# Attention weights of the last twelve units brought to keys by tokens through DRAM instead of TensorE transposes

## The chip, the cores and the metric

The kernel runs on one core of a Trainium2 chip. The metric is the device time of one execution in microseconds (us). Three runs of the kernel before gave a median of 1243.5 us (1242.62 to 1245.04).

## The reference

Three layers follow each other, all in float32. An attention over eight batches and eight heads pools its keys and values by 8 first, so that 576 queries meet 72 keys. Its output, 4608 tokens by 512 features, goes through a feed-forward layer with an ELU (512 to 2048 to 512), and that one's through a second with a softmax-weighted activation and a layer norm (512 to 1024 to 512).

```python
k_p = k.reshape(B, H, Sp, 8, D).mean(axis=3); v_p = v.reshape(B, H, Sp, 8, D).mean(axis=3)
scores = scale * q @ k_p.T
attn = exp(scores - max(scores)); attn = attn / (sum(attn) + 1e-9)
x = (attn @ v_p) as [4608, 512]
h = x @ w_in;  x = elu(h) @ w_out
h = x @ w_in2; solu = h * softmax(h); ln = (solu - mean) / sqrt(var + 1e-6) * g_ln
out = ln @ w_out2
```

## The kernel before

**Units.** The attention is done in 32 units, a unit being one batch and two heads (128 features). Four units make the 576 tokens of a batch. Unit i has the tiles q and k (128 features by 576 tokens) and v (72 keys by 128 features by 8). `att_setup` reduces k and v over the pool of 8 on VectorE (`att_kr`, line 477, and `att_vr`, line 496) and scales k on ScalarE into two diagonal blocks (`att_kc`, lines 487 and 488). `att_scores` (line 514) multiplies five blocks of 128 tokens with them; the fifth block is the last 128 of the 576 tokens and overlaps the fourth by 64. The result is ten groups of 72 scores for each of 128 tokens (two heads, five blocks; tile "es"). VectorE takes maximum and difference (lines 533, 535), ScalarE the exponential (542), VectorE the sum and its reciprocal (558 to 561), GpSimd multiplies (563).

**Keys by tokens.** The product with v needs the weights with keys on the partitions. `att_T(i, 0)` transposes the first head's four groups on TensorE into PSUM (line 573), and ScalarE copies them to the tile "a" (574). `att_T(i, 1)` does the second head's four and then the fifth block of both heads (lines 573, 574, 578, 580). `att_V` multiplies "a" with the pooled v, 64 features of one head at a time, in pieces that end at a block of 512 tokens (line 599). `att_x` brings the result to DRAM (tensor x0d) by a ScalarE copy and a DMA (613, 614), for tokens from 1536 on.

**Where the units run.** Tokens go in nine blocks of 512. The first feed-forward layer does the first three blocks as plain products (`m_h1`, `m_o1`: lines 975 and 1030), and the other six in three pairs by a form of Strassen's product with seven products in place of eight (`h_step`, line 1170, and `o_step`, line 1260). Each product there is six matmuls of 512 columns. A pair has 56 products in `h_step` and 28 steps of two in `o_step`. Every product takes one weight tile of 256 KB from a ring of 14 (`w_ring`, tile "wr", line 1162). The third pair has no attention beside it; the second layer (`z_mul`, `z_out`, lines 1367 and 1505) follows.

Attention steps are spread over the products: `att_half(n)` is called with a growing n, four steps a unit. With i = n // 4, step 0 does scores, maximum and exponential of unit i; step 1 the sums of unit i and `att_T(i - 1, 1)`; step 2 `att_V(i - 1)`, `att_x(i - 1)` and `att_setup(i + 1)`; step 3 `att_T(i, 0)`. The counter `credit` grows with each product so that the steps up to `upto(...)` are done when the outputs of `o_step` 4 are. Units 20 to 27 fall into the first pair, 28 to 31 into the second. While the last steps of a pair's `o_step` run, `sx_next` loads the next pair's blocks from x0d (line 1116, tiles sA, su, sP) and builds their sums, differences and splits into two parts (lines 1079, 1080).

**The order.** Everything up to the second layer is put in order by the planner `settle` before the program is built. It gives each instruction a cost, follows the five queues in time, and writes each engine's order down; the chip then works in that order. TensorE's products keep the order of the program, but one that is not ready may be passed by up to ten later ones (`WINDOW`). VectorE and ScalarE take what is due first. All DMAs are issued from SyncE's one queue, in the planned order; a DMA that waits there holds those behind it. Tiles have a fixed number of buffers ("es" 3, "a" 2, "cv" 2, PSUM tag "C" 2).

The second layer has a round trip through DRAM of the kind that the change uses: VectorE transposes blocks of 32 by 32 (`t_dve`, line 1454), a DMA writes them to the tensor zd (`t_store`, 1459), four DMAs bring them back with features on the partitions (`t_load`, 1466), and ScalarE and VectorE read the loaded tile in runs of 32 elements (1474, 1478).

Of the kernel before, what the change touches and what calls it, by code (L numbers as in the profile page):

```python
# [8 lines left out]
F32 = mybir.dt.float32  # L9
# [329 lines left out]
def kernel(  # L339
# [15 lines left out]
    nc = tc.nc  # L355
    P = 128
    NB, NP, _, S = qT.shape
    SK = v.shape[2]
# [12 lines left out]
    sb = ctx.enter_context(tc.tile_pool(name="sb", bufs=2))  # L371
    ps = ctx.enter_context(tc.tile_pool(name="ps", bufs=2, space=bass.MemoryType.PSUM))
    dr = ctx.enter_context(tc.tile_pool(name="dr", bufs=1, space=bass.MemoryType.DRAM))
    att = ExitStack()
    pa = att.enter_context(tc.tile_pool(name="pa", bufs=2, side="right"))
    first = ExitStack()
    p1 = first.enter_context(tc.tile_pool(name="p1", bufs=2))

    x0d = dr.tile([P, KDM, NT], F32, name="x0d")
    x1d = dr.tile([P, KDM, NT], F32, name="x1d")  # L380
    w1d = dr.tile([P, NF // 2, 7, 2, 256], F32, name="w1d")
    w3d = dr.tile([P, 7, NF // 2, 2, 256], F32, name="w3d")
    w2d = dr.tile([P, 7, 4, 512], F32, name="w2d")
    o2d = dr.tile([P, 2, 2, 4, 512], F32, name="o2d")
    zd = [dr.tile([4, P, 256], F32, name=f"zd{i}") for i in range(4)]
    ident = cst.tile([P, P], F32, name="ident")
    make_identity(nc, ident)
# [13 lines left out]
    starts = [512 * j for j in range(NBLK)]  # L401
    units = [(b, p) for b in range(NB) for p in range(NP)]
    NU = len(units)
    QT = (0, P, 2 * P, 3 * P, S - P)
    NG = 2 * len(QT)

    GROUPED = (1,2)
    NTREE = 3
    KPOOL = ()
    NPOOL = ()  # L410

    xh, xl = {}, {}
    gate = {}

    def xblk(j):
        if j not in xh:
            xh[j] = xtile(f"xh{j}")
            xl[j] = xtile(f"xl{j}")
        return xh[j], xl[j]
# [3 lines left out]
    st = {}  # L423
# [26 lines left out]
    def pool_tree(dst, src):  # L450
        n = POOL // 2
        while n > 1:
            nc.gpsimd.tensor_tensor(src[:, :, 0:n], src[:, :, 0:n], src[:, :, n:2 * n], op=ALU.add)
            n //= 2
        nc.gpsimd.tensor_tensor(dst, src[:, :, 0], src[:, :, 1], op=ALU.add)
# [25 lines left out]
    def att_kc(i):  # L481
        kp, kr = att_kv(i)[0], st.pop(("kr", i))
        if i in KPOOL:
            nc.gpsimd.tensor_scalar(kp[0:64, 0:SK], kr[0:64, :], 1.0 / (8 * POOL), None, op0=ALU.mult)
# [5 lines left out]
    def att_vr(i):  # L490
        v_t = st["kq", units[i][1]][2] if i < NP else st["ld", i][1]
        vr = att_kv(i)[1]
        if i < NTREE:
            pool_tree(vr, v_t)
# [3 lines left out]
    def att_setup(i):  # L498
        for part in (att_kr, att_kc, att_vr):
            part(i)  # L500

    def bc(x, m):
        return x.rearrange("p (a o) -> p a o", o=1).to_broadcast([P, m, SK])

    def att_scores(i, banks):

        kp, vt = st["kp", units[i][0], units[i][1]]
        q_t = st.pop(("q", i))
        st["sv", i] = []
        for t0, t1 in ((0, 2), (2, 4)) if i < NP else ((0, 3), (3, 5)):  # L510
            s = next(banks)
            ts = QT[t0:t1]
            for t, o in enumerate(ts):
                nc.tensor.matmul(  # L514
                    s[:, t * 2 * SK:(t + 1) * 2 * SK], q_t[:, o:o + P], kp, start=True, stop=True
                )
            m = 2 * len(ts)
            st["sv", i].append((2 * t0, m, s[:, 0:m * SK].rearrange("p (a k) -> p a k", k=SK)))
            yield
        st["a", i] = (pa.tile([P, NG, SK], F32, name=f"es{i}", tag="es", bufs=3), vt)  # L520

    def grouped(i):
        return i in GROUPED
# [1 line left out]
    def small(name):  # L525
        return pa.tile([P, NG], F32, name=name, tag="mx", bufs=4)

# [23 lines left out]
    def att_soft(i):  # L551
        es, vt = st["a", i]
        n = 2 * NP if i < NP else NG
        es = es[:, 0:n]
# [10 lines left out]
    def att_T(i, h):  # L565

        es, vt = st["a", i]
        if h == 0:
            st["aT", i] = pa.tile([SK, 2, S], F32, name=f"a{i}", tag="a")
        a = st["aT", i]  # L570
        pt = ps.tile([P, 512], F32, name=f"pt{i}_{h}", tag="C")
        for t in range(4):
            nc.tensor.transpose(pt[0:SK, t * P:(t + 1) * P], es[:, 2 * t + h, :], ident)  # L573
        nc.scalar.copy(a[:, h, 0:4 * P], pt[0:SK, :])
        if h == 1 and i >= NP:
            pr = ps.tile([P, 512], F32, name=f"pr{i}", tag="C")
            for g in range(2):
                nc.tensor.transpose(pr[0:SK, g * P:(g + 1) * P], es[:, 8 + g, :], ident)  # L578
            lo = 5 * P - S
            nc.scalar.copy(  # L580
                a[:, :, 4 * P:S], pr[0:SK, 0:2 * P].rearrange("s (g t) -> s g t", g=2)[:, :, lo:P]
            )

    def att_V(i, banks):

# [48 lines left out]
    def rest(part):  # L634

        kz = st["kz"]
        if part == 0:
            s = ps.tile([P, 512], F32, name="rs", tag="C")
            for p in range(NP):
                nc.tensor.matmul(  # L640
                    s[RW * (p % 2):RW * (p % 2) + RW, (p // 2) * 2 * SK:(p // 2 + 1) * 2 * SK],
                    kz[:, p, qr], kz[:, p, 0:2 * SK], start=True, stop=True,
                )
            es = st["rest"] = pa.tile([P, NG, SK], F32, name="esr", tag="es", bufs=3)[:, 0:NP]
            mx = small("mxr")[:, 0:NP]
            sv = s[:, 0:NP * SK].rearrange("p (a k) -> p a k", k=SK)
            nc.vector.tensor_reduce(mx, sv, axis=AX, op=ALU.max)
            nc.vector.tensor_tensor(es, sv, bc(mx, NP), op=ALU.subtract)
            nc.scalar.activation(es, es, AF.Exp)
        elif part == 1:  # L650
            es = st["rest"]
            sm = small("smr")[:, 0:NP]
            nc.vector.tensor_reduce(sm, es, axis=AX, op=ALU.add)
            nc.vector.tensor_scalar(sm, sm, 1e-9, float(POOL), op0=ALU.add, op1=ALU.mult)
            nc.vector.reciprocal(sm, sm)
            nc.gpsimd.tensor_tensor(es, es, bc(sm, NP), op=ALU.mult)
        elif part == 2:
            es = st.pop("rest")
            pt = ps.tile([P, 512], F32, name="ptr", tag="C")
            for g in range(NP):  # L660
                nc.tensor.transpose(pt[0:SK, g * P:(g + 1) * P], es[:, g, :], ident)
            st["rest"] = kz[0:SK, :, qr.stop:qr.stop + P]
            nc.scalar.copy(st["rest"], pt[0:SK, :].rearrange("s (g t) -> s g t", t=P))
        else:
            a = st.pop("rest")
            pv = ps.tile([P, 512], F32, name="pvr", tag="C")
            for p in range(NP):
                for h in range(2):
                    d = slice(64 * h, 64 * h + 64)
                    o = RW * (p % 2)  # L670
                    nc.tensor.matmul(
                        pv[d, p * RW:(p + 1) * RW], kz[0:SK, p, 2 * SK + 64 * h:2 * SK + 64 * h + 64],
                        a[:, 2 * (p // 2) + h, o:o + RW], start=True, stop=True,
                    )
            th, tl = (x[:, :, 0:RW] for x in xblk(1))
            src = pv[:, 0:NP * RW].rearrange("p (a t) -> p a t", t=RW)
            nc.scalar.copy(th, src)
            nc.vector.tensor_tensor(tl, src, th.bitcast(F32), op=ALU.subtract)

    def single():  # L680
        while True:
            yield ps.tile([P, 512], F32, name="at", tag="C")
# [2 lines left out]
        for _ in range(2):  # L685
            yield ps.tile([P, 512], F32, name="at2", tag=tag, bufs=4 if tag == "A" else 2)

    NSTEP = 4 * NU + 3
    nload = [0]

    def att_half(n):

        while nload[0] < min(NU, n // 4 + 3):
            att_load(nload[0])
            nload[0] += 1
        i, r = divmod(n, 4)
        before = NP <= i - 1
        if r == 0:
            if i < NU:
                for _ in att_scores(i, single()):  # L700
                    pass
                att_max(i)
                att_exp(i)
        elif r == 1:
            if i < NU:
                att_soft(i)
            if before:
                att_T(i - 1, 1)
        elif r == 2:
            if before:  # L710
                att_V(i - 1, single())
                att_x(i - 1)
            if i + 1 < NU:
                att_setup(i + 1)
        elif r == 3:
            if i < NU:
                att_T(i, 0)


# [828 lines left out]
    def startup():  # L1548
# [28 lines left out]
        def T(i):  # L1577
            att_T(i, 0)
            att_T(i, 1)
# [133 lines left out]
    def upto(j):  # L1713

        i = ((512 * (j + 1) - 1) // S) * NP + NP - 1
        return min(NSTEP, 4 * i + 7)

    goal = [upto(1), (upto(1) + upto(4)) // 2 // 4 * 4 + 3, upto(4)]
    def combo_all():
# [78 lines left out]
    pu = third.enter_context(tc.tile_pool(name="pu", bufs=1, reuse_waits="tile"))  # L1798
    prs = [4, 5, 6, 7]

    for pr in range(NTP):
        c = NPL + 2 * pr
# [216 lines left out]
    before = None  # L2019
    for key, n in seq:  # L2020
        k = (key, n)
# [18 lines left out]
        before = k  # L2040
    for n, (a, b) in enumerate(map(tiles_of, range(NPAIR))):
        if n > 1:
            c = n // 2
# [3 lines left out]
            x = [("xl", c) if c > 1 else "x1", ("S4", n - 2)]  # L2047
# [80 lines left out]
```

## Time and profile before

| | |
|---|---|
| Median of the runs | 1243.5 us |
| Profiled execution, its own time | 1244.2 us |
| Span, first to last instruction | 1242.4 us |
| TensorE busy | 1231.6 us (99%) |
| VectorE busy | 980.7 us (79%) |
| ScalarE busy | 823.1 us (66%) |
| GpSimd busy | 173.9 us (14%) |
| DMA moved | 263.31 MB, 212 GB/s |

PE is TensorE's matmul, PEld its weight load, DVE VectorE, ACT ScalarE, POOL GpSimd, SPq SyncE's queue. TensorE's matmuls overlap in the records: the duration of one is longer than the distance from its start to the next one's, so a price is read from starts. A "x" with a number is the count of instructions in a row. The clock is a share of full speed.

### The profile page before, as it was taken

To read this page: it belongs to the slowest core of one execution; us is meant where nothing else is said; L and a number is where in the kernel's file an instruction comes from. 1 tells how busy PE (TensorE), PEld (TensorE's weight loads), DVE (VectorE), ACT (ScalarE), POOL (GpSimd) and SP (SyncE) were. 2 spreads that over 40 slices of the span, in tenths; PEclk is the share of its full clock that TensorE was granted. 3 is DMA by queue.
4 is the path that set the end of the run, shared out by engine and by line. 5 is a ranking of instruction groups with operands and counts; after the bars stand their busy time and mean duration, and the time that the engine had idled before them with its cause. 6 is when DMAs were issued, how large, how long until landed. Compare 5 with 4: busy or idle time off the path is not lost.

```text
span 1242.4 us, 17361 instructions
## 1 busy us (share of the span) xinstructions
PE 1231.6 (99%) x5824; PEld 996.5 (80%) x5824; DVE 980.7 (79%) x1487; ACT 823.1 (66%) x1378; POOL 173.9 (14%) x148
## 2 busy tenths in 40 slices
PE   8999999999999999999999999999999999999998
PEld 6777787777787878788888788888888888888887
DVE  7898888888777789866788587996788787878763
ACT  7978666566667775557774477753676776767664
POOL 3554323332210010000000000000000000000000
PEclk9999999999999999999999999999999999999999
DMA  8877666676657878697766888788545444554341
GB/s 287 258 222 256 196 199 217 220 267 222 220 182 225 251 219 250 210 303 215 206 204 217 283 277 270 251 273 320 202 153 170 161 132 157 168 155 144 110 151 53
DMA packets 172841, 263.31 MB, mean 212 GB/s; under 512 B 16336, under 2 KB 88528, under 8 KB 171728
## 3 DMA queue, kind: packets, MB, share of 16 engines
q1 hardware_dynamic: 172752, 262.21, 66.2%
q8 instruction: 46, 0.75, 0.2%
q14 instruction: 43, 0.35, 0.1%
HBM read 182.46 MB, written 79.69 MB: 211 GB/s over the span
## 4 chain that ended last, share of the span: by engine, by line
PE 97%; ACT 1%; DVE 1%; POOL 0%; DMA 0%; issue 0%; ACTq 0%
PE po L1505 16%; PE hA L1170 16%; PE oA L1260 12%; PE h L975 10%; PE o L1030 10%; PE zX L1367 8%; PE zZ L1367 4%; PE oC L1260 4%; PE at L514 3%; PE at L599 3%; PE hB L1170 3%; PE oB L1260 3%; PE pt L573 2%; PE zY L1367 2%; PE pr L578 0%; PE busy L1575 0%
## 5 line engine op out<-in xcount | busy, mean ns | idle before, releaser
L1505 PE MATMUL po<-w,dhl 128*128 128x512 f32 x864 | 203.7, 392 | 0.0
L1505 PEld LDWEIGHTS po<-w,dhl 128*128 128x128 f32 x864 | 162.2, 188 | 35.1
L1260 PE MATMUL oA<-op,wr 128*128 128x512 f32 x672 | 158.2, 392 | 0.0
L1260 PEld LDWEIGHTS oA<-op,wr 128*128 128x128 f32 x672 | 125.1, 188 | 30.1 <-issue 2.9
L1250 ACT CAST op<-g 128x1024 fp32r<-128x1024 f32 x84 | 87.9, 1052 | 63.4 <-PE oA L1260 29.3
L1251 DVE TENSOR_TENSOR op<-g,op 128x1024 fp32r<-128x1024 f32 x84 | 102.6, 1227 | 24.8 <-ACT op L1250 24.3
L1170 PE MATMUL hA<-sS,wr 128*128 128x512 f32 x414 | 103.7, 392 | 0.0
L1367 PE MATMUL zX<-w,xh 128*128 128x512 f32 x288 | 100.8, 392 | 0.0
L1445 POOL TENSOR_TENSOR sc<-sc,mhalf 128x1 f32<-128x1 f32 x36 | 20.9, 586 | 558.3 <-DVE sc L1444 295.3
L896 POOL TENSOR_TENSOR wol<-wo,woh 128x512 fp32r<-128x512 f32 x48 | 75.6, 1578 | 135.7 <-ACT woh L895 122.9
L563 POOL TENSOR_TENSOR es<-es,sm 128x720 f32<-128x720 f32 x28 | 45.4, 1621 | 329.0 <-DVE sm L561 237.6
L1170 PEld LDWEIGHTS hA<-sS,wr 128*128 128x128 f32 x414 | 77.0, 188 | 17.8 <-issue 1.4
L975 PE MATMUL h<-xh,wh 128*128 128x512 f32 x192 | 78.6, 409 | 0.1
L1030 PE MATMUL o<-gh,woh 128*128 128x512 f32 x192 | 78.7, 410 | 0.0
L975 PE MATMUL h<-xh,wl 128*128 128x512 f32 x192 | 75.4, 393 | 0.7 <-POOL wl L792 0.7
L975 PE MATMUL h<-xl,wh 128*128 128x512 f32 x192 | 75.3, 392 | 0.0
L1030 PE MATMUL o<-gh,wol 128*128 128x512 f32 x192 | 75.1, 391 | 0.0
L1182 ACT COPY sp<-hA 128x512 f32<-128x512 f32 x72 | 42.2, 586 | 38.5 <-PE hA L1170 38.2
L1190 DVE SCALAR_TENSOR_TENSOR g<-ep,g 128x512 f32<-128x512 f32 x72 | 51.3, 717 | 17.7 <-ACT ep L1189 17.3
L1367 PEld LDWEIGHTS zX<-w,xh 128*128 128x128 f32 x288 | 54.1, 188 | 12.3
L1377 ACT COPY sn<-zX 128x512 f32<-128x512 f32 x54 | 31.7, 587 | 48.1 <-PE zX L1367 47.8
L1189 ACT ACTIVATE ep<-ep 128x512 f32<-128x512 f32 x96 | 59.1, 630 | 1.8
(374 smaller groups left out, 2817.3 us busy)
## 6 DMA issues: line engine op xcount, KB each, us to landing
wr<-w3d SPq DMA_DIRECT2D x168, 256.0 KB
wr<-w1d SPq DMA_DIRECT2D x161, 256.0 KB
raw<-in_w SPq DMA_DIRECT2D x32, 512.0 KB
dT<-zd SPq DMA_DIRECT2D x128, 128.0 KB
v<-in_v SPq DMA_DIRECT2D x32, 288.0 KB
x1r<-x1d SPq DMA_DIRECT2D x9, 1024.0 KB
out<-ot SPq DMA_DIRECT2D x36, 256.0 KB
raw<-in_w SPq DMA_DIRECT2D x8, 1024.0 KB
```

The source lines that it names most:

```text
L563: eng.tensor_tensor(es, es, bc(sm, n), op=ALU.mult)
L896: nc.gpsimd.tensor_tensor(ol, t[:, f % 4, :], oh.bitcast(F32), op=ALU.subtract)
L975: nc.tensor.matmul(h[:, 0:n], a[g][:, kk, fo:fo + P], x[j][:, kk, 0:n], start=(kk == 0 and m == 0), stop=(kk == KDM - 1 and m == 2), skip_ ...
L1030: nc.tensor.matmul(acc, a[:, dm * P:(dm + 1) * P], x[:, 0:n], start=(f == 0 and m == 0), stop=(f == NF - 1 and m == 2))
L1170: nc.tensor.matmul(bank, w[:, a, kk], x[:, b, kk], start=(start and m == 0), stop=(stop and m == 5), skip_group_check=True,)
L1189: gate["act"] = nc.scalar.activation(e, e, AF.Exp, scale=-1.0).ins
L1190: gate["dve"] = nc.vector.scalar_tensor_tensor(d, e, 1.0, h, op0=ALU.subtract, op1=ALU.max).ins
L1250: gate["act"] = nc.scalar.copy(o[:, 0], src).ins
L1251: gate["dve"] = nc.vector.tensor_tensor(o[:, 1], src, o[:, 0].bitcast(F32), op=ALU.subtract).ins
L1260: nc.tensor.matmul(banks[d], ws[i][:, a, d * P:(d + 1) * P], o[:, b, i], start=(start and t == 0 and i == 0 and m == 0), stop=(stop and t ...
L1367: nc.tensor.matmul(bank, x[:, o:o + P], w[:, y + k, :], start=(start and m == 0), stop=(stop and m == 5), skip_group_check=True,)
L1505: nc.tensor.matmul(po, a[:, c], b[c // 4][:, c % 4, :], start=(m == 0), stop=(m == 3 * NC2 - 1))
```

## The change

For units 20 to 31 `att_T` and `att_V` are replaced by two functions. `att_D(i)` takes its place at step 3 of unit i. It has VectorE transpose three blocks of 32 keys (0 to 31, 32 to 63, 64 to 95, of which the last has 8 keys) for all ten groups; each is written to DRAM and read back into "a", with keys on the partitions and tokens in an order of 32-token parts. `att_VB(i - 1)` comes at step 3 of unit i, one step later than `att_V` did, ahead of `att_D(i)`. It multiplies in that order, and three ScalarE copies put the tokens back; the first 512 and the last 64 tokens go to x0d in two DMAs. `att_setup(i + 1)` moves from step 2 to step 3 where unit i - 1 is one of these. The number of steps grows by one. The tile "es" gets 24 columns more, which GpSimd clears for these units, and "a" has room for 640 tokens.

```diff
+    ed = [dr.tile([3, P, NG * 32], F32, name=f"ed{i}") for i in range(3)]
+    BLOCKT = range(20, 32)
...
-        st["a", i] = (pa.tile([P, NG, SK], F32, name=f"es{i}", tag="es", bufs=3), vt)
+        e = pa.tile([P, NG * SK + 24], F32, name=f"es{i}", tag="es", bufs=3)
+        if i in BLOCKT:
+            nc.gpsimd.memset(e[:, NG * SK:], 0.0)
+        st["a", i] = (e[:, 0:NG * SK].rearrange("p (g k) -> p g k", k=SK), vt)
...
-            st["aT", i] = pa.tile([SK, 2, S], F32, name=f"a{i}", tag="a")
+            st["aT", i] = pa.tile([SK, 2, 5 * P], F32, name=f"a{i}", tag="a")
...
+    def att_D(i):
+        es, vt = st["a", i]
+        part, g, k = (list(x) for x in es.ap)
+        a = st["aT", i] = pa.tile([SK, 2, 5 * P], F32, name=f"a{i}", tag="a")
+        av = a.rearrange("k h t -> k (h t)").rearrange("k (r x) -> k r x", r=4)
+        for b in range(3):
+            n = min(32, SK - 32 * b)
+            et = pu.tile([P, NG, 32], F32, name=f"et{i}", tag="et", bufs=2)
+            nc.vector.transpose(et, bass.AP(es.tensor, es.offset + 32 * b * k[0], [part, g, [k[0], 32]]))
+            nc.sync.dma_start(out=ed[i % 3][b], in_=et.rearrange("p g c -> p (g c)"))
+            nc.sync.dma_start(
+                out=av[32 * b:32 * b + n], in_=ed[i % 3][b].rearrange("(r f) x -> f r x", r=4)[0:n]
+            )
+
+    def att_VB(i, banks):
+        es, vt = st.pop(("a", i))
+        a = st.pop(("aT", i)).rearrange("k h t -> k (h t)").rearrange("k (r t h c) -> k h r t c", r=4, h=2, c=32)
+        b, p = units[i]
+        x = sb.tile([P, 512], F32, name="xr", tag="cv", bufs=2)
+        y = sb.tile([P, 512], F32, name="xr", tag="cv", bufs=2)[:, 0:S - 512]
+        xv = x.rearrange("p (t r c) -> p t r c", r=4, c=32)
+        for r, n in ((0, 4), (2, 5)):
+            pv = next(banks)
+            for h in range(2):
+                d = slice(64 * h, 64 * h + 64)
+                nc.tensor.matmul(pv[d, 0:64 * n], vt[:, d], a[:, h, r:r + 2, 0:n], start=True, stop=True)
+            o = pv[:, 0:64 * n].rearrange("p (r t c) -> p t r c", r=2, c=32)
+            st["pv", i, r] = o
+        for r, n in ((0, 4), (2, 5)):
+            o = st.pop(("pv", i, r))
+            nc.scalar.copy(xv[:, :, r:r + 2], o[:, 0:4])
+            if n > 4:
+                nc.scalar.copy(y.rearrange("p (r c) -> p r c", c=32), o[:, 4])
+        for t, lo, hi in ((x, 0, 512), (y, 512, S)):
+            gate["x0"] = nc.sync.dma_start(out=x0d[:, p, b * S + lo:b * S + hi], in_=t).ins
...
-    NSTEP = 4 * NU + 3
+    NSTEP = 4 * NU + 4
...
-        before = NP <= i - 1
+        before = NP <= i - 1 and i - 1 not in BLOCKT
...
-            if i + 1 < NU:
+            if i + 1 < NU and i - 1 not in BLOCKT:
                 att_setup(i + 1)
         elif r == 3:
-            if i < NU:
+            if i - 1 in BLOCKT:
+                att_VB(i - 1, single())
+                if i + 1 < NU:
+                    att_setup(i + 1)
+            if i in BLOCKT:
+                att_D(i)
+            elif i < NU:
                 att_T(i, 0)
...
-        return min(NSTEP, 4 * i + 7)
+        return min(NSTEP, 4 * i + (8 if i in BLOCKT else 7))
```

## Rows read from the trace of the kernel before

**Rows 1.** The page's busy times, their shares of the span and counts:
```profile
PE 1231.6 (99%) x5824; PEld 996.5 (80%) x5824; DVE 980.7 (79%) x1487; ACT 823.1 (66%) x1378; POOL 173.9 (14%) x148
```

**Rows 2.** The page's chain that ended last, by engine:
```profile
PE 97%; ACT 1%; DVE 1%; POOL 0%; DMA 0%; issue 0%; ACTq 0%
```

**Rows 3.** TensorE's list of waits, whole span: us, times, longest:
```profile
PE pt L573 <- DVE es L563: 2.9, 2, 2.1
...
PE h L975 <- POOL wl L792: 0.7, 1, 0.7
```

**Rows 4.** Windows: us and count per engine, clock, DMA share, GB/s:
```profile
362.30:450.00 87.70, 87.70 (x435) 70.23 (x434) 67.55 (x102) 63.99 (x119) 6.64 (x4) 1.00 0.78 241
450.00:525.00 75.00, 75.00 (x375) 59.48 (x374) 66.86 (x84) 44.55 (x72) 7.88 (x4) 1.00 0.74 229
525.00:544.50 19.50, 19.50 (x88) 16.15 (x86) 12.44 (x13) 8.45 (x9) 0.00 (x0) 1.00 0.96 326
544.50:710.70 166.20, 166.20 (x775) 134.60 (x774) 121.99 (x148) 103.18 (x160) 4.42 (x3) 1.00 0.74 226
```

**Rows 5.** Timeline of TensorE around two groups of transposes: start, length, instruction:
```profile
549.95 0.60 PE L573 MATMUL pt<-ident,es 128*72 128x128 f32 x4
550.30 1.62 PE L1170 MATMUL hB<-sP,wr 128*128 128x512 f32 x6
551.76 1.52 PE L1170 MATMUL hA<-sP,wr 128*128 128x512 f32 x6
553.12 1.52 PE L1170 MATMUL hA<-sS,wr 128*128 128x512 f32 x6
...
607.16 0.60 PE L573 MATMUL pt<-ident,es 128*72 128x128 f32 x4
...
607.73 1.62 PE L1170 MATMUL hA<-sA,wr 128*128 128x512 f32 x6
609.19 1.52 PE L1170 MATMUL hA<-sV,wr 128*128 128x512 f32 x6
```

**Rows 6.** Groups by line, 365 to 700 us: busy, mean ns | idle before:
```profile
L573 PE MATMUL pt<-ident,es 128*72 128x128 f32 x96 | 14.4, 272 | 0.0
L574 ACT COPY a<-pt 72x512 f32<-72x512 f32 x24 | 13.9, 578 | 3.6 <-PE pt L573 3.5
L578 PE MATMUL pr<-ident,es 128*72 128x128 f32 x24 | 4.6, 272 | 0.0
```

**Rows 7.** Groups by line and form, whole span:
```profile
L1250 ACT CAST op<-g 128x1024 fp32r<-128x1024 f32 x84 | 87.9, 1052 | 63.4 <-PE oA L1260 29.3 <-PE oB L1260 9.9 <-PE oC L1260 9.0
L1474 ACT CAST dhl<-dT 128x1024 fp32r<-128x1024 f32 x32 | 33.3, 1040 | 4.7 <-DMA dT<-zd 4.7
...
L1454 DVE STREAM_TRANSPOSE hb<-e 128x1024 f32<-128x1024 f32 x16 | 19.9, 1244 | 3.3 <-ACT e L1435 2.4
L535 DVE TENSOR_TENSOR es<-at,mx 128x288 f32<-128x288 f32 x32 | 14.3, 451 | 0.2
```

**Rows 8.** Timeline, es of unit 27, products with v of 26 and 27:
```profile
496.47 2.16 POOL L563 TENSOR_TENSOR es<-es,sm 128x720 f32<-128x720 f32 x1 [18.03 <-DVE sm L561]
501.27 1.19 PE L599 MATMUL at<-a,vt 72*64 72x128 f32 x8
521.44 1.19 PE L599 MATMUL at<-a,vt 72*64 72x128 f32 x8
```

**Rows 9.** Window of the second layer:
```profile
863.00:1242.00 379.00, 375.44 (x1654) 307.48 (x1652) 279.94 (x492) 249.11 (x376) 20.86 (x36) 1.00 0.46 150
```

**Rows 10.** SyncE's queue, waits 340 to 711 us: us, times, longest:
```profile
SPq L1162 <- PE hA L1170: 92.0, 84, 5.0
```

**Rows 11.** Timeline of a round trip through DRAM in the second layer:
```profile
893.79 0.38 SPq L1459 DMA_DIRECT2D zd<-hb  x1
...
896.71 1.76 SPq L1466 DMA_DIRECT2D dT<-zd  x4
...
901.61 1.03 ACT L1474 CAST dhl<-dT 128x1024 fp32r<-128x1024 f32 x1
```

**Rows 12.** Timeline at the second pair's start:
```profile
544.46 1.23 DVE L1080 TENSOR_TENSOR sP<-sP 128x1024 fp32r<-128x1024 f32 x1
...
547.22 1.52 PE L1170 MATMUL hB<-sP,wr 128*128 128x512 f32 x6
```

More of the change, by code (lines that the diff above doesn't have):

```diff
@@ L377 @@
     p1 = first.enter_context(tc.tile_pool(name="p1", bufs=2))
+    QT = (0, P, 2 * P, 3 * P, S - P)
+    NG = 2 * len(QT)
     x0d = dr.tile([P, KDM, NT], F32, name="x0d")
@@ L403 @@
     NU = len(units)
-    QT = (0, P, 2 * P, 3 * P, S - P)
-    NG = 2 * len(QT)
     GROUPED = (1,2)
     NTREE = 3
+    BLOCKT = range(20, 32)
     KPOOL = ()
@@ L643, in rest @@
                 )
-            es = st["rest"] = pa.tile([P, NG, SK], F32, name="esr", tag="es", bufs=3)[:, 0:NP]
+            es = st["rest"] = pa.tile([P, NG * SK + 24], F32, name="esr", tag="es", bufs=3)[:, 0:NP * SK].rearrange("p (g k) -> p g k", k=SK)
             mx = small("mxr")[:, 0:NP]
```

## The prediction

> **What bounds the kernel now.** I read the busy shares first: TensorE works 1231.6 of 1242.4 us, the others 79% and less [rows 1]. The chain of waits says the same: 97% of the chain that ended last is TensorE [rows 2]. Then I asked what TensorE waited for: five entries from 2.9 down to 0.7 us [rows 3], none in the stretch that the change touches, where it is busy throughout [rows 4]. Last came the stretches. Units 20 to 31 lie in the first two block pairs, 362 to 711 us. There TensorE is busy without a gap at a granted clock of 1.00 (the 2.4 GHz level), VectorE 77% (362.3 to 450) and 89% (450 to 525), and the DMA engines 78%, 74%, then 96% just ahead of the second pair [rows 4]. So in these stretches each us of TensorE work taken out is a us of time, as long as no other engine, queue or transfer becomes late by it.
>
> **What the change takes off TensorE.** Per unit it drops ten transposes, in a group of four and one of four and two. Their durations overlap with their neighbours', so I price them by starts. The group of four starts at 549.95 and the next product at 550.30: 0.35 us; that product then takes 1.46 us to its successor, where a plain one takes 1.36 (551.76 to 553.12): 0.10 more. The group of six: 607.16 to 607.73 is 0.57, and again 0.10 behind it. Together 1.12 us a unit [rows 5]. The trace has 96 + 24 transposes in the stretch, ten for each of twelve units [rows 6], so 12 x 1.12 = 13.4 us leave the path.
>
> The Trainium skill, page "TensorE: Matmul & The Clock Gate", Part 4 (PE-mode transpose), gives about 275 ns for a transpose in a kernel's context; the trace agrees on the duration of one (272 ns), but the starts are some 90 ns apart. By the page's figure as a price, 120 of them would be worth 33 us and the time 1211 us; I go by the starts.
>
> **What it puts on TensorE.** att_VB has four matmuls as att_V has, 576 columns a head as before (2 x 256 and 2 x 320). New is the order in which they read: runs of 32 elements instead of one long run. No row shows TensorE reading so. The nearest one is ScalarE's, which reads 1024 columns in such runs in 1040 ns and contiguous ones in 1052 [rows 7]: I take nothing. From above: if runs halved the rate, the eight recorded pieces of a unit (1.19 us [rows 8]) would cost about 1.1 us more, 12 x 1.1 = 13 us, all of the gain. From below a gain is excluded, since columns and matmuls are the same.
>
> **VectorE** gets three transposes of 320 columns a unit. Scaled down from its 1244 ns for 1024 columns one takes 0.39 us; 288 columns of another operation take 0.45 [rows 7]. I take 0.45, 1.35 us a unit. From 450 to 525 us lie 3.7 units (one each 20.2 us [rows 8]): 66.9 + 5.0 = 71.9 us of work in 75.0 - 4.1 = 70.9 us. It is 1 us overfull there, with 7 us of spare time in the 19.5 us behind it [rows 4]. Its splits for the output products are made up to six tiles ahead, 2.7 us of TensorE each, so most of this is covered; bounds 0 and 4 us (no cover, and waits for the two "et" buffers on top), I take 0.5. Att_setup moves one step back: its reductions and two ScalarE scalings are as many as before, each with a unit of time to spare. ScalarE loses two copies of 0.58 us [rows 6] and a short one a unit and gains a third copy in att_VB; it is no bound either way. GpSimd gets one memset of 24 columns, next to an idle queue.
>
> **DMA and SyncE's queue.** A unit writes 3 x 160 KiB and reads 72 x 5 KiB: 0.86 MB in six transfers. The trace's only transfers of this form, the last stage's round trip of transposed blocks in runs of 1 KB, lie in a stretch with a share of 0.46 at 150 GB/s, 326 GB/s for a full share [rows 9]; so 2.6 us of all 16 engines a unit. From 362 to 450: 0.78 x 87.7 + 4.35 x 2.6 = 79.7 us in 82.8 (96%); from 450 to 525: 65 in 70.9 (92%). Before, 19.5 us at 96% and 326 GB/s went by with TensorE full [rows 4]. Nothing, then, but little cover is left; were the packets half as dear again, the first stretch would be 2.6 us short. The weight ring has 14 slots of one product each, so a load is asked for 14 x 1.36 = 19 us ahead: SyncE mostly waits for TensorE to free a slot, 92 us in 84 waits [rows 10]. A load that waits at the queue's head for its store, about 3 us, delays the ring loads and the x0 writes behind it by that, inside those 19 us.
>
> **The new round trip** sits between es and att_VB. In the last stage a store is issued at 893.79, its loads at 896.71, and the data is used at 901.61: 7.8 us with four loads behind each other [rows 11]. For unit 27 es is ready at 496.47 + 2.16 = 498.6 and its product with v starts at 521.44 [rows 8]: 22.8 us, of which three transposes and 8 us leave some 13. In the second pair four units share 166 us [rows 4], twice the distance. The wait is covered, and TensorE may take up to ten later pieces first in the order that the planner writes.
>
> **The pair's boundary** is the thin spot. P2's split ends at 544.46 + 1.23 = 545.7 and is used at 547.22: 1.5 us [rows 12]. Att_VB(27) stays at the last step before the loads that build the next pair, but unit 28's store and loads (2.6 us of DMA) now come in the stretch that is at 96% already. Bounds 0 and 2.6 us; I take 0.4.
>
> **The sum.** The profiled execution took 1244.2 us, 0.7 more than the median shown. 1244.2 - 13.4 + 0.5 + 0.4 = 1231.7; less the 0.7, **1231 us**.
>
> **Rivals.**
> 1. *Crowding in the first pair* (B): VectorE overfull, DMA at 96%, and the boundary together give back 3 to 10 us: 1234 to 1241. For it: the shares above. Against it: ring and tiles ahead; TensorE did not wait at 96% of DMA. The Trainium skill, page "VectorE: DVE Perf Modes", Rules for kernel authors, has a full 128 x 128 transpose on TensorE where PSUM will do as its destination, and VectorE's for blocks of 32. Taken as a price of this kernel that speaks against the change only if VectorE were the bound; the trace has it at 77 to 89% beside a full TensorE.
> 2. *No change* (C): TensorE reads runs of 32 at half the rate: 1242 to 1245. For it only that no row shows it.
> 3. *Slower* (D): the round trip lands later than the order written by the planner assumes. TensorE works in that order, so it stands still at att_VB, and its weight ring, splits and the next scores wait with it. It decides at a lateness of 1.12 us a unit; at 3 us the time is 1244 + 12 x 1.9 = 1266, at 2 us 1254. For it: SyncE's one queue with six more waits a unit, full DMA engines. Against it: some 13 us of cover, and in the second pair more than 25.
> 4. *The transposes come back elsewhere* (the change doesn't do what it says): if units other than these or the first group only were moved, half the gain: 1237. The diff takes both groups out for all twelve, so I count it with B.
>
> **Chances.** Forecast 0.71, B with 4 0.15, C 0.04, D 0.10. The forecast's own range is 1229 to 1234. With B inside, 1228.5 to 1240 leaves out some of its end, C and D, under 2 in 10; the low end has the group's price 10% higher and no give-back. Bound for "same" is 0.2%, 2.5 us: what a measurement can tell. Faster 0.86, same 0.04, slower 0.10.
>
> **What would show it.** No TensorE transposes after the first pair's start; products 1.36 us apart where they were; att_VB's pieces as long as att_V's, or C holds. TensorE's list of waits in the two pairs stays empty; an entry "at <- DMA a" is D, "hB/hA <- VectorE" at the second pair's start is the boundary. Pair one shorter by 9.0 us, pair two by 4.5. VectorE up by some 16 us in all, one transpose near 0.4 us; ScalarE down by some 13; DMA share about 0.9 in pair one. The prediction is wrong if TensorE's idle time in the two pairs is over 3 us, or if att_VB costs more than att_V did.

## The result and the profile after

The changed kernel takes **1229.96 us** (median of 5 runs, 1228.7 to 1230.83); the kernel before took 1243.42 beside it (1242.62 to 1245.04). The ratio is 0.989, 95% interval 0.9876 to 0.9905. The forecast was 1231.0, with its own range 1229 to 1234. The profiled executions took 1244.2 us (span 1242.4) and 1229.96 us (span 1228.2).

The page after: busy times, the chain that ended last, the DMA line.

```profile
PE 1218.8 (99%) x5704; PEld 986.9 (80%) x5704; DVE 992.5 (81%) x1523; ACT 811.1 (66%) x1354; POOL 176.9 (14%) x160
...
DMA packets 181961, 273.63 MB, mean 223 GB/s; under 512 B 18416, under 2 KB 96624, under 8 KB 180848
...
PE 97%; ACT 1%; DMA 1%; DVE 1%; POOL 0%; issue 0%; ACTq 0%; POOLq 0%
```

TensorE has 120 instructions and 12.8 us less than in [rows 1] and is still the whole chain, as in [rows 2]. VectorE has 36 instructions more (the block transposes), ScalarE 24 fewer. The transfers of before came to 263.31 MB; 10.3 MB more is 12 x 0.86.

The two largest of the four entries in TensorE's list of waits after, whole span (us, times, longest), and the windows that answer to [rows 4] (us, busy us and count of PE, PEld, DVE, ACT and POOL, clock, DMA share, GB/s):

```profile
PE pt L579 <- DVE es L569: 2.3, 2, 1.2
PE busy L1623 <- POOL ident masks.py:199: 1.4, 1, 1.4
...
```
```profile
360.70:449.00 88.30, 88.30 (x419) 70.96 (x419) 76.02 (x122) 63.05 (x114) 6.61 (x9) 1.00 0.93 291
449.00:514.90 65.90, 65.90 (x315) 52.21 (x314) 62.09 (x81) 37.44 (x60) 6.91 (x6) 1.00 0.92 285
514.90:534.40 19.50, 19.50 (x88) 16.13 (x87) 17.69 (x21) 9.23 (x12) 1.39 (x1) 1.00 0.94 323
534.40:696.10 161.70, 161.70 (x735) 131.48 (x734) 126.07 (x161) 99.03 (x152) 5.89 (x4) 1.00 0.83 259
```

In the two pairs TensorE is busy for as long as each window lasts, at a clock of 1.00, and its list of waits has no entry there. VectorE is at 86% and then 94% of the first two windows, the DMA engines at 0.93 and 0.92: both are fuller than before. ScalarE is a little emptier. None of them made TensorE wait.

The table cuts each profiled execution at the first product of each block pair (us; the last column runs to the end of the span). Its rows are before, after and the experiments that moved no work ahead of the first pair.

| kernel | first product | pair 1 | pair 2 | pair 3 | rest |
|---|---|---|---|---|---|
| before | 361.52 | 182.98 | 166.24 | 152.35 | 379.31 |
| after | 360.74 | 173.64 | 161.73 | 152.76 | 379.33 |
| dead transposes | 359.99 | 182.89 | 165.78 | 152.60 | 379.54 |
| pair 1 only | 361.71 | 174.17 | 165.80 | 153.06 | 379.26 |
| pair 2 only | 362.37 | 183.02 | 162.14 | 152.75 | 379.52 |
| three stores | 360.07 | 180.08 | 164.78 | 152.32 | 380.45 |
| product a step earlier | 362.08 | 173.66 | 161.66 | 152.86 | 379.34 |

The change takes 9.34 us from pair 1 and 4.51 from pair 2, 13.85 together. The first product's place differs by up to 2.4 us between kernels that are the same up to there, so a single profile tells 1 us or less only inside a pair, where the unchanged pairs agree within about 0.5 us (pair 3 within 0.75).

### The profile page after: what moved, and what is told of

Its sections match the earlier page's. It is cut to its first block, busy times and chain, and to the rows that moved or that the text cites. A ratio compares the mean times of both kernels' runs of the same rounds, so it can differ in the third digit from the quotient of the medians.

```text
span 1228.2 us, 17259 instructions
## 1 busy us (share of the span) xinstructions
PE 1218.8 (99%) x5704; PEld 986.9 (80%) x5704; DVE 992.5 (81%) x1523; ACT 811.1 (66%) x1354; POOL 176.9 (14%) x160
## 4 chain that ended last, share of the span: by engine, by line
PE 97%; ACT 1%; DMA 1%; DVE 1%; POOL 0%; issue 0%; ACTq 0%; POOLq 0%
PE po L1553 16%; PE hA L1218 15%; PE oA L1308 13%; PE h L1023 11%; PE o L1078 10%; PE zX L1415 8%; PE zZ L1415 4%; PE oC L1308 4%; PE at L517 3%; PE oB L1308 3%; PE hB L1218 3%; PE zY L1415 2%; PE at L641 2%; PE pt L579 1%; PE at L615 1%; PE busy L1623 1%
## 5 line engine op out<-in xcount | busy, mean ns | idle before, releaser
L1033 ACT ACTIVATE e<-h 128x512 f32<-128x512 f32 x48 | 28.7, 597 | 46.4 <-PE h L1023 46.3
```

## Experiments

**1. The transposes back, nothing else.** Theory: the gain is TensorE's time for the transposes, and the new work on VectorE, SyncE and the DMA engines is hidden. Rival: part of the gain comes from something else that became shorter, or part is lost to the new work.

```diff
+    def dead_T(i, h):
+        es, vt = st["a", i]
+        pt = ps.tile([P, 512], F32, name=f"pt{i}_{h}", tag="C")
+        for t in range(4):
+            nc.tensor.transpose(pt[0:SK, t * P:(t + 1) * P], es[:, 2 * t + h, :], ident)
+        if h == 1:
+            pr = ps.tile([P, 512], F32, name=f"pr{i}", tag="C")
+            for g in range(2):
+                nc.tensor.transpose(pr[0:SK, g * P:(g + 1) * P], es[:, 8 + g, :], ident)
...
+            if i - 1 in BLOCKT:
+                dead_T(i - 1, 1)
...
                 att_D(i)
+                dead_T(i, 0)
```

> The changed kernel with its ten TensorE transposes a unit put back at their old steps, read by nobody: the ScalarE copies stay out, the round trip through DRAM stays in. Theory (the gain is TensorE's time for the transposes and nothing else; all added work is hidden): 12 x 1.12 = 13.4 us come back, 1243.4 us, within 1.5. Rival (the gain comes from relieved ScalarE, free PSUM banks or a luckier order): the time stays below 1237. A time above 1245 would say that the added VectorE, DMA and queue work costs something that the gain hides.

1244.15 us, ratio 1.0 (0.999 to 1.0009). The window of its first pair, and the groups of the transposes put back:

```profile
360.00:542.90 182.90, 182.70 (x902) 147.07 (x901) 157.78 (x225) 108.44 (x184) 14.18 (x16) 1.00 0.91 282
```
```profile
L608 PE MATMUL pt<-ident,es 128*72 128x128 f32 x96 | 14.4, 272 | 0.2
L612 PE MATMUL pr<-ident,es 128*72 128x128 f32 x24 | 4.6, 273 | 0.0
```

Both pairs are back at the length of before within 0.5 us, though all the block transposes, stores and loads are made as well. The gain is TensorE's time; the added work costs nothing that this measurement can tell (its interval is some 1.2 us to either side). The busy time of the groups is 19.0 us and the time that they cost is 13.3 (182.89 - 173.64 and 165.78 - 161.73): the durations overlap.

**2 and 3. One pair alone.** Theory: 1.12 us a unit wherever the unit lies. Rival: crowding in pair 1 or at its end, so that pair 1 alone gives less and pair 2 alone more than its share.

```diff
-    BLOCKT = range(20, 32)
+    BLOCKT = range(20, 28)
```
```diff
-    BLOCKT = range(20, 32)
+    BLOCKT = range(28, 32)
```

> Only units 20 to 27, those of the first block pair, go by DRAM. Theory: 8 x 1.12 = 9.0 us less than before, 1234.4; the first pair lasts 173.6 us as in the changed kernel, the second 166.2 as before. Rival (crowding at the boundary of the pairs costs something, because unit 28 also transfers there): the second pair starts earlier than in the changed kernel by 1 us or more.

> Only units 28 to 31 go by DRAM. Theory: 4 x 1.12 = 4.5 us less than before, 1238.9; first pair 183.0 us, second 161.7. The 0.7 us by which the first product starts earlier in the changed kernel comes back here only if it is the planner's order of the start (the tiles' sizes are the same), then 1238.2. Rival: the gains of the two pairs don't add, and this one is over 6 us or under 3.

Units 20 to 27: 1235.31 us, ratio 0.9932 (0.9917 to 0.9947). Units 28 to 31: 1240.69, ratio 0.9972 (0.9963 to 0.9982). By the table pair 1 is 8.81 us shorter in the one and pair 2 4.10 in the other, 1.10 and 1.03 a unit. So the sizes follow the number of units. By the medians the gains are 8.4 and 3.0 us; the interval of the second reaches from 2.2 to 4.6, so the median alone would not have ruled out its rival (under 3), and the reading rests on the pairs' lengths. The second kernel lies 1.8 us above what was expected; 0.85 of it stands ahead of the first pair (362.37 against 361.52) and 0.4 each in the units' gain and in pair 3, which is within what single profiles differ by.

**4. Three stores for one.** How near was the crowding? Each block is stored twice more, to buffers that nobody reads.

```diff
+    e2 = [dr.tile([3, P, NG * 32], F32, name=f"e2{i}") for i in range(6)]
...
+            for m in range(2):
+                nc.sync.dma_start(out=e2[2 * (i % 3) + m][b], in_=et.rearrange("p g c -> p (g c)"))
```

> Each block is stored twice more, to tensors that nobody reads: 0.98 MB more a unit, 3.1 us of all DMA engines at the changed kernel's 291 GB/s for 93%. In the first pair's first 154 us 143 us of DMA work become 168: 14 us short. Theory (the DMA engines' share is a limit, and the weight ring's 14 tiles give 19 us of lead once): TensorE begins to wait in the first pair, 2 to 14 us in all, 1232 to 1244. Rival (a share near 1 is no limit, since packets overlap): no change, 1229 to 1231, the share passes 1.0 and the rate 330 GB/s.

1240.8 us, ratio 0.9976 (0.9965 to 0.9987): 10.8 of the 13.5 us are gone. Its windows, three rows of TensorE's waits and one of VectorE's:

```profile
360.10:449.00 88.90, 88.22 (x415) 70.45 (x414) 72.96 (x116) 63.03 (x112) 6.31 (x8) 1.00 0.88 291
449.00:514.90 65.90, 62.46 (x295) 49.14 (x294) 63.85 (x84) 34.03 (x54) 6.24 (x7) 1.00 0.99 309
514.90:540.10 25.20, 24.57 (x110) 19.29 (x110) 12.23 (x14) 9.00 (x13) 1.39 (x1) 1.00 1.03 360
```
```profile
PE oA L1311 <- DMA wr<-w3d: 1.6, 2, 0.9
PE hA L1221 <- DVE sP L1131: 1.6, 1, 1.6
PE at L618 <- DMA a<-ed: 1.0, 1, 1.0
...
DVE su L1180 <- DMA sA<-x0d: 6.5, 1, 6.5
```

The DMA share reaches 0.99 and 1.03, and now what the DMA engines feed is late by a little: weights, a product with v, and the second pair's split, for which VectorE waited 6.5 us on a load. SyncE's queue is late too. Its largest wait from 360 to 515 us, in the changed kernel and then here:

```profile
SPq L1210 <- PE oA L1308: 15.9, 27, 1.6
...
SPq L600 <- DVE et L599: 22.9, 14, 4.6
```

In the changed kernel the queue mostly waits for TensorE to free a weight slot. Here it waits for VectorE's transposes, with everything else behind them. Pairing the loads of the weight ring with the products in their order, a load is issued 18 to 23 us ahead of its product from 449 to 515 us in the changed kernel, and 5 to 14 us here. So what B and D describe does appear when the stores are tripled, which puts about 2 us more of all 16 engines on each unit (25 us over the two pairs, by shares and lengths of the windows). Whether the engines' share, the six more issues a unit on one queue or the buffers "et" that are held longer set the limit, this run doesn't tell.

**5. The product with v one step earlier.** If its place were tight, taking a step of the round trip's time away would show.

```diff
                 att_x(i - 1)
-            if i + 1 < NU and i - 1 not in BLOCKT:
+            if i - 1 in BLOCKT:
+                att_VB(i - 1, single())
+            if i + 1 < NU:
                 att_setup(i + 1)
         elif r == 3:
-            if i - 1 in BLOCKT:
-                att_VB(i - 1, single())
-                if i + 1 < NU:
-                    att_setup(i + 1)
```

> The changed kernel with att_VB and att_setup one step earlier, where att_V stood: about three products, 4 us. In the changed kernel a unit's last load is issued 6 to 8 us ahead of att_VB and lands some 3 us later, so 3 to 5 us of cover are left. Theory (TensorE may pass a piece that is not ready, so the place in the program doesn't matter as long as the planner knows the round trip): 1230, within 1.5, and no wait of TensorE for the loaded tile over 0.5 us. Rival (the cover is needed on the chip, since the round trip takes longer there than planned): TensorE waits for the loads up to 1 us a unit, 1234 to 1242.

1229.89 us, ratio 0.9885 (0.9869 to 0.9902): no change. Unit 27's product with v, in this kernel:

```profile
512.68 1.19 PE L615 MATMUL at<-a,vt 72*64 72x256 f32 x8
```

The product runs at the same place as in the changed kernel (512.69, below): in the planned order a step of the program sets its place only loosely. Its last load is issued at 507.08, no earlier than there (506.40). This run doesn't tell how much time the round trip has left.

**6 and 7. More units.** If a unit gives 1.12 us wherever TensorE is the bound, starting from unit 16 or 12 should give more. The "et" buffers don't exist ahead of the first pair, so the blocks of units up to 20 lie in a tile of the tag "cv".

```diff
-    BLOCKT = range(20, 32)
+    BLOCKT = range(16, 32)
...
+        big = sb.tile([P, 3, NG, 32], F32, name=f"et{i}", tag="cv", bufs=2) if i < 21 else None
...
-            et = pu.tile([P, NG, 32], F32, name=f"et{i}", tag="et", bufs=2)
+            et = big[:, b] if big is not None else pu.tile([P, NG, 32], F32, name=f"et{i}", tag="et", bufs=2)
```

> Units 16 to 19 go by DRAM too; they lie in the first layer's plain products. Their three transposed blocks (and unit 20's) use one tile of the tag cv, since the pool of the others does not exist there yet. Theory (each unit is worth its transposes' TensorE time wherever TensorE is full): 4 x 1.15 = 4.6 us less than the changed kernel, 1225.4. Rival (VectorE at 85% and the tag cv in that stage give it back): 1228 or more.

> Units 12 to 19 go by DRAM too, as in the run from unit 16. Theory: 8 x 1.15 = 9.2 us less than the changed kernel, 1220.8; the first stage ends 9 us earlier, the pairs last as long as in the changed kernel. Rival (VectorE, 270 us of 321 before and 12 more after, or the tile of tag cv holds TensorE up): 1224 or more, with waits of TensorE for VectorE or ScalarE between 200 and 350 us.

From 16: 1250.84 us, ratio 1.0057 (1.0042 to 1.0072). From 12: 1274.33, ratio 1.0245 (1.023 to 1.026). The timeline of the first around TensorE's largest wait (in brackets: the wait and what ended it); then the two largest waits of the second:

```profile
348.71 1.19 PE L616 MATMUL at<-a,vt 72*64 72x256 f32 x8
...
367.99 0.37 SPq L1120 DMA_DIRECT2D su<-x0d  x1
...
374.95 1.23 DVE L1139 TENSOR_TENSOR su<-su,sA 128x1024 f32<-128x1024 f32 x1 [6.05 <-DMA su<-x0d]
...
381.08 2.08 PE L1219 MATMUL hA<-sP,wf 128*128 128x512 f32 x4 [22.42 <-DVE sP L1129]
```
```profile
PE at L616 <- DMA a<-ed: 25.2, 3, 17.8
PE hA L1219 <- DVE sP L1129: 16.6, 1, 16.6
```

The row names VectorE's split, but the split comes behind the load of "su", the last of the first pair's inputs. The expectation of experiment 8 blames the buffer of "su", a "cv" tile too. Its load is issued 19.3 us behind unit 19's product with v (the first row), though, and that distance is 19 to 22 us in every kernel of this case. What is late is that product: 324.08 in the changed kernel, 348.71 here. From unit 12 the products with v wait for the loads of the round trip as well: this is rival D, seen at 25 us, with borrowed buffers.

**8 and 9. The same with buffers of their own kind.** The blocks of units up to 20 lie in two tiles of the tag "es".

```diff
+        big = [
+            pa.tile([P, NG * SK + 24], F32, name=f"et{i}_{m}", tag="es", bufs=3)[:, 0:640].rearrange("p (b g c) -> p b g c", b=2, c=32)
+            for m in range(2)
+        ] if i < 21 else None
...
-            et = pu.tile([P, NG, 32], F32, name=f"et{i}", tag="et", bufs=2)
+            et = big[b // 2][:, b % 2] if big else pu.tile([P, NG, 32], F32, name=f"et{i}", tag="et", bufs=2)
```

> The run from unit 16 again, with the transposed blocks of units 16 to 20 in two tiles of the tag es in place of one of the tag cv. In that run TensorE stood 22 us at the first pair's start for the load of su, which is a cv tile too and got its buffer only after the blocks of the last units had been stored. Theory (the borrowed buffers were the whole cause): 1225.4, within 1.5, no such wait. Rival (a unit's round trip of 14 to 17 us is too long for units that lie 9 to 18 us apart in the first layer): TensorE waits for the loaded tile or for the pair's first splits, 1230 or more.

> The same from unit 12. In its run with cv tiles TensorE stood 25 us at three att_VB for their loads (one of 17.8) and 17 us at the first pair's start. Theory (buffers): 1220.8 to 1223. Rival (round trip longer than the distance of the units there): waits for the loaded tile stay, 3 us or more in all, and the time is 1226 or more.

From 16: 1235.59 us, ratio 0.9944 (0.9927 to 0.996). From 12: 1236.25, ratio 0.9945 (0.9927 to 0.9963). The borrowed "cv" buffers were most of the loss, but not all of it; TensorE's waits for the round trip from unit 12 are gone with them. The first kernel's timeline:

```profile
355.61 0.72 PE L1222 MATMUL hA<-sP,wf 128*128 128x512 f32 x2
...
364.19 2.08 PE L1222 MATMUL hA<-sP,wf 128*128 128x512 f32 x4 [7.85 <-DVE sP L1132]
```

The first layer is 5.1 us shorter (355.61 against 360.74), about what four units' transposes should make it, and then TensorE stands for 7.85 us: the first pair's inputs need the output of unit 19, and its product with v starts at 331.39, 7.3 us later than in the changed kernel.

**10 and 11. Attention of the first layer ended sooner.** The planner's goal for attention steps is set eight steps higher in the middle part, and its rate in the last part reaches its goal two tiles earlier; the buffers are those of experiments 8 and 9.

```diff
-    goal = [upto(1), (upto(1) + upto(4)) // 2 // 4 * 4 + 3, upto(4)]
+    goal = [upto(1), (upto(1) + upto(4)) // 2 // 4 * 4 + 11, upto(4)]
...
-            rate = max(goal[j] - step, 0) / (2.0 * (NF - 4 if j == 0 else NF if j < 2 else NF - 6))
+            rate = max(goal[j] - step, 0) / (2.0 * (NF - 4 if j == 0 else NF if j < 2 else NF - 8))
```

> From unit 12 with own tiles, and the units of the first layer's last block spread so that they end two of its sixteen steps (11 us) sooner: the middle goal is 67 in place of 59 and the rate's divisor 16 in place of 20. In the run before, the first layer ended 8.4 us sooner than in the changed kernel, as eight units' transposes are worth, but TensorE then stood 11 us at the first pair's splits, whose loads need unit 19's output. Theory (that output's lateness is the cause): the wait is under 2 us, 1221 to 1223. Rival (the units are now denser, VectorE or the round trip comes late inside the first layer): waits of the same size move there, 1228 or more.

> The same from unit 16; there the wait was 7.9 us at the first pair's splits, after a first layer 5.1 us shorter. Theory: 1225 to 1227 with a wait under 2 us. Rival: 1230 or more, with waits inside the first layer.

From 16: **1225.46 us** (1224.57 to 1226.47), ratio 0.9847 (0.9831 to 0.9864), 4.5 us under the changed kernel, as 4 x 1.12 makes it (5.2 by the kernels before that ran beside each). Its two largest TensorE waits, and the first products of pairs 1 and 2:

```profile
PE busy L1627 <- POOL ident masks.py:199: 1.4, 1, 1.4
PE pt L579 <- DVE es L569: 1.1, 2, 0.8
```
```profile
355.32 1.64 PE L1222 MATMUL hA<-sP,wf 128*128 128x512 f32 x6
...
529.30 1.52 PE L1222 MATMUL hA<-sP,wr 128*128 128x512 f32 x6
```

The first pair starts 5.4 us earlier than in the changed kernel, without a stand, and lasts 173.98 us. From 12: 1237.0 (1232.95 to 1242.18), ratio 0.9949 (0.9933 to 0.9964). Its profiled execution, the longest of nine with 1242.18 us, still waits:

```profile
PE hA L1222 <- DVE sP L1132: 7.0, 1, 7.0
PE o L1082 <- ACT x1s L1095: 2.4, 1, 2.4
PE at L619 <- DMA a<-ed: 2.2, 1, 2.2
```

The starts of unit 19's product, of the load of "su" and of the first pair's first product that needs the late split tell the kernels apart (us):

| kernel | unit 19's product | load of "su" | first pair | TensorE's stand there |
|---|---|---|---|---|
| after | 324.08 | 345.69 | 360.74 | none |
| 6, from 16, "cv" | 348.71 | 367.99 | 381.08 | 22.42 |
| 8, from 16, own | 331.39 | 352.61 | 364.19 | 7.85 |
| 11, from 16, sooner | 320.06 | 339.33 | 355.32 | none |
| 10, from 12, sooner | 332.18 | 351.21 | 366.85 | 7.04 |

The first pair runs 32 to 37 us behind unit 19's product in all of them. Experiment 11 brought that product forward, and the stand went; experiment 10 didn't. Why unit 19 stays late there was not settled.

## Why the prediction was right, step by step

**The bound, and the price by starts: right.** TensorE gave back what was taken off it: 1.17 us a unit in pair 1 and 1.13 in pair 2, for 1.12 worked out from [rows 5]. Experiment 1 loses the same when the transposes return, and in experiments 2, 3 and 11 the gain scales with the number of units. By durations the groups of [rows 6] would have been worth 19.0 us.

**TensorE reading runs of 32: nothing, as taken.** Rival C is out. Pieces of a product with v among plain products, before and after:

```profile
578.18 1.52 PE L1170 MATMUL hA<-sS,wr 128*128 128x512 f32 x6
579.63 1.20 PE L599 MATMUL at<-a,vt 72*64 72x64 f32 x8
580.75 1.65 PE L1170 MATMUL hA<-sS,wr 128*128 128x512 f32 x6
582.24 1.54 PE L1170 MATMUL hA<-sP,wr 128*128 128x512 f32 x6
...
566.98 1.52 PE L1218 MATMUL hA<-sS,wr 128*128 128x512 f32 x6
568.43 1.19 PE L615 MATMUL at<-a,vt 72*64 72x256 f32 x8
569.55 1.67 PE L1218 MATMUL hA<-sS,wr 128*128 128x512 f32 x6
571.06 1.55 PE L1218 MATMUL hA<-sP,wr 128*128 128x512 f32 x6
```

The eight recorded pieces last 1.19 us as in [rows 8]. By starts, after: 1.45, 1.12 and 1.51 make 4.08, less two plain products of 1.36 is 1.36 for the eight. Before it is 1.34 in the same way.

**VectorE: hidden, its price 10% low.**

```profile
L598 DVE STREAM_TRANSPOSE et<-es 128x320 f32<-128x320 f32 x36 | 17.4, 497 | 1.6 <-POOL es L569 1.6
```

497 ns for one where 450 was taken, 17.4 us in all. The page's busy time rose by 11.8 us only, where some 16 were forecast; the durations of its groups add up to 15.6 more, but records of neighbours overlap and the page counts such time once. (ScalarE fell by 12.0, forecast some 13.) The windows after don't match the forecast's stretches one for one. Taken together, from the first pair's start to 514.9, VectorE worked 138.1 us in 154.2, and the 19.5 us behind that took 17.7 where it had been 12.4: there was room, and the give-back of 0.5 was nothing.

The Trainium skill, page "VectorE: DVE Perf Modes", Rules for kernel authors, has a full 128 x 128 transpose go to TensorE where PSUM will do as its destination. By this kernel's traces the measurement decides the other way: TensorE was the bound, and the way by VectorE and DRAM took 1.1% off.

**DMA: right.** The work of all 16 engines is 0.93 x 88.3 + 0.92 x 65.9 = 142.7 us where [rows 4] have 0.78 x 87.7 + 0.74 x 75.0 = 123.9 for the same part of the pair: 2.4 us for each of eight units, 2.6 predicted. At 0.93 TensorE stayed full, and the weight loads kept their lead of some 20 us, as predicted (19). In experiment 4, at 0.99, they didn't.

**The round trip: the mechanism right, its cover far too large.** This is the term that was mis-sized. The prediction left "some 13" us. Unit 27 after:

```profile
492.52 2.19 POOL L569 TENSOR_TENSOR es<-es,sm 128x720 f32<-128x720 f32 x1 [7.32 <-DVE sm L567]
495.72 0.50 DVE L598 STREAM_TRANSPOSE et<-es 128x320 f32<-128x320 f32 x1
...
501.64 0.51 DVE L598 STREAM_TRANSPOSE et<-es 128x320 f32<-128x320 f32 x1
...
506.40 0.29 SPq L600 DMA_DIRECT2D a<-ed  x1
...
512.69 1.19 PE L615 MATMUL at<-a,vt 72*64 72x256 f32 x8
```

From "es" to the product are 18.0 us (494.71 to 512.69), where the prediction counted on the 22.8 of the kernel before. The three transposes are spread over 6 us, with other work of VectorE between them, and the third takes the buffer that the first one's store reads. The last load is issued 10.7 us after the first transpose (10.7 to 14 over the eight units of pair 1), 6.3 us ahead of the product (6.2 to 8.2). How long such a load takes shows in experiment 4, where TensorE waited for one:

```profile
499.03 0.33 SPq L603 DMA_DIRECT2D a<-ed  x1
...
502.34 1.19 PE L618 MATMUL at<-a,vt 72*64 72x256 f32 x8 [0.98 <-DMA a<-ed]
```

That is 3.3 us from issue to use, so 3 to 5 us were left (an estimate: no load's landing is in the trace of the changed kernel). The prediction added up the three transposes and the 8 us of [rows 11] as if buffers were free and the DMA engines idle; [rows 9] had them at 0.46.

**The boundary: nothing, 0.4 taken.** P2's split and its use at the second pair's start after:

```profile
533.80 1.23 DVE L1128 TENSOR_TENSOR sP<-sP 128x1024 fp32r<-128x1024 f32 x1
...
537.11 1.52 PE L1218 MATMUL hB<-sP,wr 128*128 128x512 f32 x6
```

The split ends at 535.03, 2.1 us ahead of its use; in [rows 12] it was 1.5.

**The sum.** The two give-backs of 0.9 us were nothing, and the gain in the pairs was 13.85 for 13.4; with 0.4 us more in pair 3 and 0.8 less ahead of the first pair, the profiled execution fell by 14.2 us. The median fell by 13.46. The forecast was 1.0 us high: most of it is the 0.9 of the two give-backs.

## What to carry to other kernels

Price an instruction that leaves a full engine by the starts around it, with and without it, and not by its duration: here that was 13.4 us against 19.0, and 13.5 was measured. Work can be moved off the bound engine as long as nothing else becomes late in that stretch, and the margin is found by adding more of the same cost: at a DMA share of 0.93 nothing was late, and with about twice the added traffic (a share of 0.99, and one queue that issues late) four fifths of the gain were gone. Extending such a change needs a look at what the borrowed buffers delay and at who needs the last unit's output, and when; with both mended, four more units gave their 4.5 us, and eight did not.

## What the runs showed of the hardware

Behind a long stand TensorE was slower for a while. In experiment 8 it had been full at a granted clock of 1.00, stood for 7.85 us, and then:

```profile
345.00:356.00 11.00, 11.00 (x55) 9.23 (x53) 6.32 (x10) 5.73 (x10) 2.27 (x5) 1.00 0.38 116
...
364.20:367.00 2.80, 2.80 (x7) 2.24 (x8) 2.77 (x3) 2.23 (x3) 0.00 (x0) 0.50 1.05 404
367.00:372.00 5.00, 5.00 (x18) 3.98 (x17) 4.97 (x5) 1.05 (x1) 0.00 (x0) 0.71 0.91 350
372.00:380.00 8.00, 8.00 (x37) 6.64 (x36) 3.67 (x9) 3.82 (x7) 1.39 (x1) 1.00 0.35 102
```

The clock column (the third from the end) is 0.50, the 1.2 GHz level, for 2.8 us, 0.71 over the next 5, then 1.00 again: 2.8 x 0.50 + 5 x 0.29 = 2.9 us of full-speed work lost on top of the stand. Together that is 10.7 us; experiment 8 is 10.1 above experiment 11, which has no stand there. Behind the stands of experiments 6 and 7 (22.4 and 17.8 us) the clock was 0.55 over 5 us and 0.50 over 4. And the DMA engines' throughput at a full share was no fixed number: 404 GB/s here at 1.05, 309 GB/s at 0.99 in experiment 4.
